# An allocation order that moves a decode kernel's large buffer by 128 bytes

## The chip, the cores and the metric

The kernel runs on one core of one Trainium2 chip. The metric is the device time of one execution in microseconds. SBUF, the core's working memory, has 128 partitions; an address below is a byte offset within each partition, and a tile lies at the same offset in all of its partitions. HBM is the main memory, where inputs and outputs are. Engines: PE multiplies matrices, DVE and ACT do elementwise work, POOL and SP here mainly issue transfers. Transfers are carried by 16 DMA engines, whichever engine issues them.

## The reference

One decode step (one token) of a transformer block, forward and backward, in bfloat16. x and h are vectors of 448 elements.

```
h   = x + A(layernorm(x))          # 16 heads of 256 over 8 K/V heads, window of the last 4096 of 32768 positions, then wo
h2  = h + B(layernorm(h))          # (x @ w_gate) * (x @ w_up) @ w_down, 448 -> 1792 -> 448
outputs: h2, and for grad_out the gradients of x, k_cache, v_cache, wq, wo, w_gate, w_up, w_down
```

The gradients of k_cache and v_cache have the caches' shape, (1, 8, 32768, 256) each, and are zero outside the window of 4096. Writing these zeros is most of what the kernel moves.

## The kernel before

**Memory.** Three pools are opened: `const`, `small` and one in PSUM. Tiles of `const` are laid out one after another in the order in which the code allocates them. The first is `BIG` (L53), 128 x 88,832 bfloat16, 177,664 bytes in each partition, which is 694 x 256. It is cut by hand: ten slots of 16,384 bytes (`SLOT` elements; `slot(k)` and `half(k, h)`, L117 to L121) and a tail of 13,824 bytes. K, V, the weights, the products on their way and the results on their way out all live in BIG at some time. The second is `zeros` (L65), 16,384 bytes in each partition. Then come `Mt` (L110), the identity and mask tiles, the layernorm tiles, `qT`, `pT_all` (L306) and `oT_f` (L307): 32 float32 to a partition, 128 bytes. In the program as built, BIG starts at byte 16,512 of each partition (64.5 x 256), zeros at 194,176 (758.5 x 256), oT_f at 222,432, and the last tile ends 256 bytes below the top of SBUF.

**Transfers.** SP issues the two loads of wq (L64) and then the fills (`fill`, L71): a fill takes 16 of the zero rows, in partitions 32 to 92 by steps of 4, and writes each of them many times over, 16,384 bytes (`ZW` elements) a row, to the region of an output that lies outside the window. There are 15 such fills for whole regions (L76 to L79). The last region is dealt out in pieces (`deal`, `deal_all`, `deal_rest`), the last of them by POOL. All other transfers are issued by POOL (`IO`): loads of K and V rows (16,384 bytes to a partition, or halves of 8,192; `load_window`, L144), of weights (`load_wo`, `load_wd`, L461, L491), and stores of the finished K and V gradients (L730) and weight gradients (`outer`, L618). Fills and POOL's transfers share the 16 DMA engines.

**Work.** For each of the 8 K/V heads g, `moments(g)` (L375) multiplies K rows by the softmax weights and accumulates products with V in PSUM, with the next head's scores between; at its end L410 writes four columns of oT_f. After the loop, L479 reads oT_f (forward output projection), and L582 reads it again in the backward part. The last loop (L702) forms the gradients of K and V head by head, writes them into slots of BIG and stores them. The order of this work is that of the code, with the loads ordered by `io_load` (L137).

Of the kernel before, what the change touches and what calls it, by code (L numbers as in the profile page):

```python
# [8 lines left out]
f32 = mybir.dt.float32  # L9
# [31 lines left out]
def kernel(  # L41
# [7 lines left out]
    const = ctx.enter_context(tc.tile_pool(name="const", bufs=1))  # L49
    small = ctx.enter_context(tc.tile_pool(name="small", bufs=1))  # L50
    ps = ctx.enter_context(tc.tile_pool(name="ps", bufs=1, space=bass.MemoryType.PSUM))

    BIG = const.tile([128, SIZE], bf16)  # L53
    x_bf = BIG[0:1, 6 * SLOT:6 * SLOT + D]
    S_.dma_start(out=x_bf, in_=A_x.rearrange("a b d -> (a b) d"))
    go_bf = BIG[0:1, 6 * SLOT + 512:6 * SLOT + 512 + D]
    S_.dma_start(out=go_bf, in_=grad_out.rearrange("a b d -> (a b) d"))
# [3 lines left out]

    wq_sb = BIG[:, 4 * SLOT:4 * SLOT + NI * HQ]
    for c0, c1 in ((0, 4 * HQ), (4 * HQ, NI * HQ)):
# [53 lines left out]
    def slot(k):  # L117
        return BIG[:, k * SLOT:(k + 1) * SLOT]

    def half(k, h):  # L120
        return BIG[:, (2 * k + h) * SLOT // 2:(2 * k + h + 1) * SLOT // 2]  # L121

# [181 lines left out]
        S_.activation(out=dst, in_=t[:], func=ACT.Copy, scale=scale)  # L304

    pT_all = const.tile([128, G, T, 2], bf16)  # L306
    oT_f = const.tile([128, 32], f32)  # L307
    kbar = const.tile([128, 32], f32)
    dh2_bc = const.tile([128, D], bf16)
    d_hh = const.tile([128, FC], f32)  # L310
# [4 lines left out]
    def ring(k):  # L315
        return BIG[:, SIZE - (k + 1) * 1024:SIZE - k * 1024]

# [448 lines left out]
```

## Time and profile before

| | us |
|---|---|
| median of 3 runs | 788.1 |
| lowest and highest of them | 788.04, 788.3 |
| the profiled execution | 786.81 |
| its span, from first to last instruction | 784.9 |

The profile is of one execution. A line of its third part gives, for each DMA queue, the number of packets, the megabytes, and the time that the packets took as a share of 16 DMA engines over the span. The same lines can be had for any stretch of the span; the share is then of 16 engines over that stretch. Of the queues, q1 is the one that SP feeds, q0 the one that POOL feeds; q8 and q14 fetch instructions. A transfer of one contiguous row is one packet here, but for short rows, of which two can form one. The completion of a transfer is told by packets of 4 bytes. A table of stages gives the busy time of each engine in a stretch, the granted clock of PE as a share of full speed, the busy share of the DMA engines, and GB/s.

### The profile page before, as it was taken

How to read it: one execution, taken by the hardware profiler on the slowest of the kernel's cores; microseconds unless marked ns; L12 is line 12 of the kernel's file. 1: busy time of each engine (PE TensorE's matmuls, PEld its weight loads, DVE VectorE, ACT ScalarE, POOL GpSimd, SP SyncE). 2: the span in 40 equal slices, each digit the busy share in tenths (PEclk: the TensorE clock that was granted, in tenths of full speed). 3: DMA queues.
4: the chain of work that ended last, by engine and by line, in shares of the span. 5: the costliest groups of instructions: out<-in, count | busy, mean ns of one | idle time of the engine just before them, and what ended most of it. 6: DMA issues, size and time to landing. Idle time of an engine off the chain costs nothing.

```text
span 784.9 us, 10845 instructions
## 1 busy us (share of the span) xinstructions
PE 472.8 (60%) x4375; PEld 263.8 (34%) x4420; DVE 401.5 (51%) x1169; ACT 188.5 (24%) x277; POOL 42.3 (5%) x86
## 2 busy tenths in 40 slices
PE   4798898899998631313258897639392889700000
PEld 4654564565554320203134343314141334100000
DVE  5477677677767212295724556436856655600000
ACT  0322322321220000126024453315140444400000
POOL 3000000000000000100000001000100000000000
PEclk9998998999999755555555555555555555555555
DMA  9999999999999999999999999999999999999997
GB/s 355 425 427 430 427 425 430 427 425 430 423 430 429 429 430 432 428 428 432 426 431 426 427 426 422 423 411 427 429 413 429 427 423 423 427 421 427 426 426 297
DMA packets 25106, 330.67 MB, mean 421 GB/s; under 512 B 2669, under 2 KB 2671, under 8 KB 4468
## 3 DMA queue, kind: packets, MB, share of 16 engines
q1 hardware_dynamic: 14557, 231.15, 69.4%
q0 software_dynamic: 10496, 98.83, 30.0%
q8 instruction: 34, 0.56, 0.3%
q14 instruction: 15, 0.12, 0.0%
q10 hardware_dynamic: 4, 0.00, 0.0%
HBM read 49.38 MB, written 280.59 MB: 420 GB/s over the span
## 4 chain that ended last, share of the span: by engine, by line
PE 46%; DMA 17%; DVE 15%; issue 7%; ACT 2%; POOL 1%; POOLq 0%; DVEq 0%; ACTq 0%
PE MT L389 14%; PE d_ps L723 10%; PE tr L332 9%; DMA BIG<-in_B_w_down_dram 7%; DMA out_dram<-BIG 6%; DMA BIG<-in_A_wq_dram 3%; DVE BIG L575 2%; PE sT L337 2%; DMA BIG<-in_A_k_cache_dram 2%; DVE BIG L558 1%; PE acc L392 1%; PE acc L395 1%; DVE zeros L406 1%; PE dp L337 1%; DVE BIG L282 1%
## 5 line engine op out<-in xcount | busy, mean ns | idle before, releaser
L389 PE MATMUL MT<-BIG 128*128 128x512 bf16 x467 | 141.7, 412 | 2.0 <-DVE BIG L385 0.2
L385 DVE TENSOR_SCALAR BIG<-BIG,pf 128x256 bf16<-128x256 bf16 x512 | 114.9, 282 | 27.9 <-PE MT L389 24.8
L723 PE MATMUL d_ps<-BIG 32*128 32x512 bf16 x256 | 118.9, 620 | 9.8 <-ACT BIG L718 5.4
L332 PE MATMUL tr<-ident_bf,BIG 128*128 128x128 bf16 x1024 | 117.1, 268 | 1.8 <-DVE Mt L282 0.8
L282 DVE CAST BIG<-d_ps 128x512 bf16<-128x512 f32 x128 | 88.2, 691 | 52.5 <-PE d_ps L723 52.0
L280 ACT COPY BIG<-tr 128x1024 bf16<-128x1024 bf16 x64 | 64.8, 1012 | 161.0 <-PE tr L332 161.0
L332 PEld LDWEIGHTS <-BIG 128*128 128x128 bf16 x1024 | 79.1, 118 | 40.7 <-issue 40.1
L280 ACT CAST BIG<-d_ps 128x512 bf16<-128x512 f32 x128 | 74.8, 587 | 52.7 <-PE d_ps L723 52.7
L282 DVE COPY BIG<-tr 128x1024 bf16<-128x1024 bf16 x64 | 44.3, 692 | 50.1 <-PE tr L332 50.1
L392 PEld LDWEIGHTS <-BIG 128*128 128x128 bf16 x512 | 42.3, 99 | 52.9 <-issue 16.9
L392 PE MATMUL acc<-pT_all,BIG 128*128 128x2 bf16 x512 | 45.0, 164 | 16.6 <-DVE kbar L411 15.0
L337 PEld LDWEIGHTS <-BIG 128*128 128x128 bf16 x1024 | 39.7, 104 | 40.5 <-DVE BIG L282 19.8
L389 PEld LDWEIGHTS <-BIG 128*128 128x128 bf16 x512 | 40.8, 103 | 24.6 <-issue 18.6
L723 PEld LDWEIGHTS <-BIG 32*128 32x128 bf16 x256 | 27.5, 124 | 56.8 <-issue 56.7
L395 PE MATMUL acc<-pT_all,BIG 128*128 128x2 bf16 x512 | 44.3, 164 | 0.0
L395 PEld LDWEIGHTS <-BIG 128*128 128x128 bf16 x512 | 30.1, 96 | 0.9
L506 DVE CUSTOM_DVE_ANT_0 dh_bc<-BIG,dh_bc 128x448 bf16<-128x448 bf16 x14 | 8.7, 625 | 39.5 <-DMA BIG<-in_B_w_down_dram 39.3
L337 PE MATMUL dp<-doT,BIG 128*128 128x2 bf16 x512 | 24.6, 169 | 7.0 <-DVE BIG L282 5.5
L530 PE MATMUL y<-BIG,hh_bf 128*1 128x448 bf16 x14 | 5.9, 566 | 31.5 <-DMA BIG<-in_B_w_down_dram 28.1
L718 ACT CAST BIG<-R_ps 128x512 bf16<-128x512 f32 x8 | 4.7, 585 | 82.9 <-PE R_ps L716 82.9
L337 PE MATMUL sT<-qT,BIG 128*128 128x2 bf16 x512 | 22.5, 165 | 0.8 <-DVE BIG L282 0.6
L640 DVE CUSTOM_DVE_ANT_0 BIG<-BIG,Mt 128x2048 bf16<-128x2048 bf16 x7 | 15.7, 2288 | 12.1 <-DMA BIG<-in_A_wq_dram 12.1
(185 smaller groups left out, 373.0 us busy)
## 6 DMA issues: line engine op xcount, KB each, us to landing
out_dram<-zeros SPq DMA_DIRECT2D x15, 14336.0 KB, 151.1
out_dram<-BIG POOLq DMA_DIRECT2D x16, 2048.0 KB, 38.2
BIG<-in_A_v_cache_dram POOLq DMA_DIRECT2D x8, 2048.0 KB, 23.6
BIG<-in_A_k_cache_dram POOLq DMA_DIRECT2D x12, 1024.0 KB, 14.2
out_dram<-zeros SPq DMA_DIRECT2D x1, 6144.0 KB
out_dram<-BIG POOLq DMA_DIRECT2D x6, 896.0 KB, 42.9
BIG<-in_A_k_cache_dram POOLq DMA_DIRECT2D x2, 2048.0 KB, 24.1
out_dram<-BIG POOLq DMA_DIRECT2D x3, 1024.0 KB, 49.6
```

The costliest lines, as they stand in the source:

```text
L280: S_.copy(out=out, in_=in_)
L282: V_.tensor_copy(out=out, in_=in_)
L332: P_.transpose(tr[:, i, dh, :], x_at(g, 4 * q + i)[:, dh * 128:(dh + 1) * 128], ident_bf[:])
L337: P_.matmul(out_ps[:, 4 * q + i, :], lhsT=xt[:, i, dh, :], rhs=vecT[:, 4 * g + dh:4 * g + dh + 3:2], start=(dh == 0), stop=(dh == 1))
L385: V_.tensor_scalar(out=pk[:, i, h, :], in0=K[:, t, :], scalar1=pf[:, t, h:h + 1], scalar2=None, op0=ALU.mult)
L389: P_.matmul(MT[hf][:], lhsT=v_at(g, t)[:, hf * 128:(hf + 1) * 128], rhs=pk[:, i, :, :].rearrange("p h d -> p (h d)"), start=(t == 0), stop ...
L392: P_.matmul(acc[:, 2 * hf:2 * hf + 2], lhsT=v_at(g, t)[:, hf * 128:(hf + 1) * 128], rhs=pT_all[:, g, t, :], start=(t == 0 and hf == 0), st ...
L395: mm = P_.matmul(acc[:, 4 + dk:7 + dk:2], lhsT=K[:, t, dk * 128:(dk + 1) * 128], rhs=pT_all[:, g, t, :], start=False, stop=(t == T - 1), s ...
L506: V_.tensor_tensor_reduce(out=dh_bc[:], in0=wd_sb[:, m - m0, :], in1=dh2_bc[:], scale=1.0, scalar=0.0, op0=ALU.mult, op1=ALU.add, accum_ou ...
L575: V_.tensor_tensor_reduce(out=wg_sb[:, 0:D], in0=parked.get(b, wo_b(b)), in1=dh_bc[:], scale=1.0, scalar=0.0, op0=ALU.mult, op1=ALU.add, a ...
L640: V_.tensor_tensor_reduce(out=wq2[i], in0=wq2[i], in1=dq_bc[:, i % 2, :], scale=1.0, scalar=0.0, op0=ALU.mult, op1=ALU.add, accum_out=Pq[: ...
L723: mm = P_.matmul(d_ps[:].rearrange("p w d -> p (w d)"), lhsT=rows[32 * k:32 * k + 32, a, :], rhs=R[32 * k:32 * k + 32, :], start=True, sto ...
```

## The change

The tile oT_f is allocated ahead of BIG and no longer behind pT_all. Nothing else in the code differs, and no instruction uses it earlier or later than before. Its 128 bytes now come first in the pool, so BIG, zeros and the tiles from Mt to pT_all begin 128 bytes further on: BIG at 16,640 (65 x 256) and zeros at 194,304 (759 x 256). Tiles from kbar on, and the pools behind, stay where they are.

```diff
     ps = ctx.enter_context(tc.tile_pool(name="ps", bufs=1, space=bass.MemoryType.PSUM))
 
+    oT_f = const.tile([128, 32], f32)
     BIG = const.tile([128, SIZE], bf16)
     x_bf = BIG[0:1, 6 * SLOT:6 * SLOT + D]
...
     pT_all = const.tile([128, G, T, 2], bf16)
-    oT_f = const.tile([128, 32], f32)
     kbar = const.tile([128, 32], f32)
```

## The prediction

> **What bounds the kernel now.** I read the page's first three parts, then the table of stages, then the transfers of single stretches, because a change of addresses alone can only act through whatever sets the end.
>
> ```profile
> span 784.9 us, 10845 instructions
> PE 472.8 (60%) x4375; PEld 263.8 (34%) x4420; DVE 401.5 (51%) x1169; ACT 188.5 (24%) x277; POOL 42.3 (5%) x86
> DMA  9999999999999999999999999999999999999997
> DMA packets 25106, 330.67 MB, mean 421 GB/s; under 512 B 2669, under 2 KB 2671, under 8 KB 4468
> q1 hardware_dynamic: 14557, 231.15, 69.4%
> q0 software_dynamic: 10496, 98.83, 30.0%
> q8 instruction: 34, 0.56, 0.3%
> q14 instruction: 15, 0.12, 0.0%
> HBM read 49.38 MB, written 280.59 MB: 420 GB/s over the span
> ```
>
> No engine is busy for more than 60% of the span, while the 16 DMA engines are at 9 tenths or more in every slice but the last. Queue 1 holds the zero fills that SP issues and the first weight loads, queue 0 everything that POOL issues. The stages say the same with the engines beside it (columns: stretch, length, busy time of PE, PEld, DVE, ACT and POOL with their instructions, granted clock, DMA share, GB/s):
>
> ```profile
> 0.00:20.00 20.00, 8.58 (x43) 8.36 (x44) 11.61 (x29) 1.59 (x3) 6.02 (x20) 1.00 0.92 356
> 20.00:640.00 620.00, 425.69 (x4139) 240.09 (x4181) 362.96 (x1100) 163.65 (x237) 32.26 (x59) 0.68 1.01 427
> 640.00:690.00 50.00, 38.57 (x196) 15.38 (x196) 26.94 (x41) 23.26 (x38) 3.38 (x6) 0.50 1.01 423
> 690.00:770.00 80.00, 0.00 (x0) 0.00 (x0) 0.00 (x0) 0.00 (x0) 0.63 (x1) 0.50 1.01 427
> 770.00:784.90 14.90, 0.00 (x0) 0.00 (x0) 0.00 (x0) 0.00 (x0) 0.00 (x0) 0.50 0.60 252
> ```
>
> From 20 to 770 us the DMA engines are full (share 1.01; a little over 1 because one packet's record overlaps the next). The compute engines do nothing after 690 us; what remains is transfers. So about 95 us separate the last arithmetic from the end, and the end comes when the bytes are out. Time is the number of rows times the time per row, over 16 engines.
>
> **The change part by part.** No instruction, transfer, wait or loop is added, removed or reordered: the same tile is allocated earlier. Two things follow, addresses on the DMA side and addresses on the engine side.
>
> *Engine side.* BIG, zeros and the tiles after them up to pT_all lie 128 bytes further on, with unchanged shapes and distances within each tile. I cost this at nothing. What hides it is the transfers that run on after 690 us: an engine's work would have to grow by tens of microseconds to reach the end. Without that cover, each 1% on DVE's 401.5 us would be 4 us.
>
> *DMA side.* Practically every row of data that this kernel moves has one end in BIG or in zeros, at 128 bytes past a multiple of 256 (BIG starts at byte 16,512 of each partition, and all the large offsets into it are multiples of 256). Afterwards these ends lie on multiples of 256. The question is whether a row pays for its misplaced start. The trace has no row of this size that is known to be placed otherwise, so I bound the cost from both sides by what a row costs beyond its bytes. Four stretches, each with one size alone on queue 0: 16,384-byte loads of K and V (40 to 43 us), 12,544-byte weight loads (252 to 262), 5,376-byte stores (399 to 403), and the 4-byte completion marks (769 to 779).
>
> ```profile
> q0 software_dynamic: 40, 0.66, 50.9%
> q1 hardware_dynamic: 39, 0.64, 49.7%
> ```
> ```profile
> q0 software_dynamic: 114, 1.43, 33.4%
> ```
> ```profile
> q0 software_dynamic: 80, 0.43, 25.8%
> ```
> ```profile
> q0 software_dynamic: 46, 0.00, 0.3%
> ```
>
> The last column is the share of 16 engines over the stretch, so a row takes share x 16 x length / count:
> - 16,384 B: 0.509 x 48 us / 40 = 610.8 ns for loads; 0.497 x 48 / 39 = 611.7 ns for the fills on queue 1 beside them.
> - 12,544 B: 0.334 x 160 us / 114 = 468.8 ns.
> - 5,376 B: 0.258 x 64 us / 80 = 206.4 ns.
> - 4 B: 0.003 x 160 us / 46 = 10.4 ns, and with the rounding of the share 8.7 to 12.2 ns.
>
> The second and third give a slope of (468.8 - 206.4) / 7,168 = 0.0366 ns a byte and a fixed part of 206.4 - 5,376 x 0.0366 = 9.6 ns a row. Put into the same line, 16,384 bytes come to 609 ns, as seen. Hence the bounds:
> - Upper: a row that starts in the middle of a 256-byte block touches 65 blocks where 64 would do, and carries half a block, 128 bytes, for nothing: 128 x 0.0366 = 4.7 ns. The fixed 9.6 ns has room for that.
> - Lower: nothing. The fixed part belongs to a packet of any kind. The 4-byte marks, which can't carry 128 wasted bytes in this sense, also take about 10 ns.
>
> The number of rows is 25,106 - 2,669 under 512 bytes - 34 - 15 of instruction fetch = 22,388. The upper price gives 22,388 x 4.7 / 16 = 6.6 us. If only rows read from SBUF pay (written to HBM: 280.59 of 329.97 MB, 85%), it is 5.6 us. Below nothing is not excluded by the rows either: the row's mean in a stretch of fills alone is a little above the 611 ns of the clean stretch, and that part could grow. In 412 to 444 us
>
> ```profile
> DMA packets 847, 13.66 MB, mean 427 GB/s; under 512 B 13, under 2 KB 13, under 8 KB 13
> q1 hardware_dynamic: 845, 13.63, 100.1%
> q8 instruction: 2, 0.03, 0.4%
> ```
>
> there are 832 fill rows at 1.001 x 512 us / 832 = 616 ns, 4.3 ns more than 611.7. So the ends are -6.6 us (all rows pay now and stop paying) and +6.0 us (that excess doubles: 4.3 x 22,388 / 16).
>
> I take -6.0 us, between the two ways of counting who pays. I choose the price over nothing since the 9.6 ns is on every row in proportion to rows and not bytes, which is where such a cost would sit, and since with DMA full for 750 us whatever a row saves arrives at the end undiminished. I do not think the trace settles it: loads, whose SBUF end is the destination, and fills, whose SBUF end is the source, cost the same, so either both ends pay alike or neither does.
>
> [...]
>
> **The sum.** The profiled execution took 786.81 us, 1.9 us more than its span of 784.9; the median of the runs is 788.1, 1.3 us above it. 786.81 - 6.0 = 780.8, and 1.3 more gives 782.1 us for the median. Nothing takes the place of the saved time: the next bound is the arithmetic at 690 us.
>
> **The rivals.**
>
> *The start costs nothing.* The 9.6 ns is the price of any packet. For it: the 4-byte marks, and loads and fills alike. Against it: only that no aligned row of this size is there to compare. The time stays at 788.1, with less than 0.2% (1.6 us, about what a measurement of this kernel can tell from no change, 786.5 to 789.7) either way. A layout that is not as the change says would come to the same.
>
> *The rows collide.* Now a row's SBUF end and its HBM end are half a block out of step. Once both are in step, the 16 engines open their blocks together, and the excess over the clean row grows. The place is the stretches where fills and stores run side by side; there the excess exists already, as in 669 to 674 us:
>
> ```profile
> q0 software_dynamic: 65, 1.06, 49.9%
> q1 hardware_dynamic: 65, 1.06, 49.9%
> ```
>
> 0.499 x 80 us / 65 = 614.2 ns for stores and fills alike. It decides from 1.2 ns on the mean row (1.2 x 22,388 / 16 = 1.7 us); with the excess doubled it costs 6.0 us and gives 794.1. For it: the excess is real and varies by stretch. Against it: no row ties it to the place of a start, and the cleanest stretch has loads and fills mixed.
>
> *More than the half block.* If the excess of 4.3 ns itself comes of the misplaced start and goes too, another 6 us fall away: 776 us. For it: the excess is on fills alone too. Against it: the stretch of 40 to 43 us has hardly any, with the same starts.
>
> **How the numbers follow.** The forecast, 781 to 783.5 us: 0.50. Nothing: 0.32. Collision: 0.14. More than the half block: 0.04. Faster by over 0.2% is the first and the last together, 0.54; within 0.2% is 0.32; slower 0.14. The range leaves out the last two cases, whose chances add up to 0.18: it goes from 779.5, a little beyond the upper price, to 789.5, the upper edge of no change. The likeliest case's own range is 781 to 783.5.
>
> **What would show it.** With the forecast, the 40 loads and 39 fills of a clean stretch take about 606 ns a row instead of 611, the 5,376-byte stores 202 instead of 206, the share of queue 1 falls by some 0.7% of itself for the same 231.15 MB, and the GB/s of 20 to 640 us rise from 427 to about 430. If only rows read from SBUF pay, fills fall and loads stay. With the rival of no cost, every one of these rows keeps its duration. With the collision, the clean rows keep 611 and the means of the stretches rise above 616. The prediction is wrong if the fixed part of a row stays at 9 to 10 ns; the 4-byte marks should not move in any case.

## The result, and the profile after

The changed kernel takes 779.34 us (median of 4 runs, 779.24 to 779.54) beside 788.2 for the kernel before in its 4 runs (788.04 to 789.26): ratio 0.9885 with a 95% interval of 0.9868 to 0.9902. It is faster by 8.9 us. The forecast was 6.0, and 779.34 lies 0.16 us below the range. The direction was right and the size too small. The mechanism, as it turns out, is another one than the forecast's: the boundary of 256 bytes matters (779.2 to 779.3 us with both tiles on it, 788.2 to 789.1 with both off it, by the two kernels and three of the experiments), but not by a cost that each row carries (a clean row of 16,384 bytes takes 611 ns before and after), so that the number came out near the range is luck.

The changed kernel's page, the lines that answer to those shown of before:

```profile
span 777.7 us, 10890 instructions
DMA  9999999999999999999999999999999999999998
DMA packets 25106, 330.67 MB, mean 425 GB/s; under 512 B 2669, under 2 KB 2671, under 8 KB 4468
q1 hardware_dynamic: 14557, 231.15, 69.6%
q0 software_dynamic: 10496, 98.83, 30.2%
q8 instruction: 34, 0.56, 0.3%
```

The packets and bytes are the same to the last one. Each share is of a shorter span: queue 1's packets took 0.694 x 784.9 = 544.7 us per engine before and 0.696 x 777.7 = 541.3 now, queue 0's 235.5 and 234.9. So the rows themselves took 4.0 us less, of which 3.4 on queue 1 (a share has one decimal, so each of the four products is good to 0.4 us). The records of the single packets, added up, give 4.7 us less, of which 3.6 on queue 1. The stages (columns as in the prediction):

```profile
20.00:640.00 620.00, 431.73 (x4206) 241.84 (x4204) 365.08 (x1105) 167.28 (x243) 32.25 (x59) 0.68 1.01 429
640.00:690.00 50.00, 33.17 (x177) 13.25 (x174) 23.97 (x36) 19.66 (x33) 4.00 (x7) 0.50 1.01 430
690.00:770.00 80.00, 0.00 (x0) 0.00 (x0) 0.00 (x0) 0.00 (x0) 0.00 (x0) 0.50 1.01 430
```

The DMA engines are as full as before, at 429 to 430 GB/s in place of 427, 423 and 427. Engine work is unchanged; it ends before 690 us as it did.

**A single row costs what it did.** Three stretches of the changed kernel with one size alone on queue 0: 16,384-byte loads (40 to 43 us, with fills beside them), 12,544-byte loads (250 to 260), 5,376-byte stores (396 to 400):

```profile
q1 hardware_dynamic: 38, 0.62, 48.4%
q0 software_dynamic: 38, 0.62, 48.4%
...
q0 software_dynamic: 113, 1.42, 33.1%
...
q0 software_dynamic: 85, 0.46, 27.4%
```

By share x 16 x length / count these are 611.4 ns for loads and fills alike, 468.7 and 206.3. Before they were 611, 468.8 and 206.4. The fixed 9.6 ns of a row did not move by more than the rounding of these shares.

**What moved is the mean of the fill rows late in the run.** For a mixed stretch I take the time of one fill row as share x 16 x length / (bytes / 16,384), good to about 0.5 ns here. Queue 1 of the kernel before in four stretches, 320 to 360, 440 to 500, 520 to 560 and 690 to 750 us:

```profile
q1 hardware_dynamic: 854, 13.73, 80.1%
...
q1 hardware_dynamic: 1041, 16.76, 66.0%
...
q1 hardware_dynamic: 641, 10.24, 59.9%
...
q1 hardware_dynamic: 1018, 16.38, 64.3%
```

and of the changed kernel in 440 to 500 and 690 to 750 us:

```profile
q1 hardware_dynamic: 1028, 16.53, 64.4%
...
q1 hardware_dynamic: 1038, 16.71, 64.9%
```

Before: 611.7, 619.4, 613.4, 617.4 ns. After: 612.8 and 610.9. The excess over the clean 611 comes, goes and comes again in the kernel before, and between 690 and 750 us, where no compute engine works, the change removes all of it.

After 400 us the fill rows are slowest where a load from HBM comes in among the stores. Two loads of wq do so in the second half, issued at 503.5 and 555.0 us; their rows stand below, under the last experiment. Queue 1 in 500 to 520 us, before and after:

```profile
q1 hardware_dynamic: 329, 5.36, 67.6%
```
```profile
q1 hardware_dynamic: 336, 5.49, 64.0%
```

These are 661 and 611 ns a row. By the records of single packets, the excess of queue 1's 16,384-byte rows over 611 ns adds up to 5.7 us per engine before and 2.0 now, and 1.7 of the 3.7 between them falls in the 61.5 us in which these two loads are under way (23.2 and 38.3). In 20 to 400 us, with the loads of K, V and most weights, the two kernels are alike: 613.1 and 613.6 ns.

**The engines also end together.** The last stretches of the kernel before:

```profile
770.00:775.00 5.00, 0.00 (x0) 0.00 (x0) 0.00 (x0) 0.00 (x0) 0.00 (x0) 0.50 0.95 404
775.00:780.00 5.00, 0.00 (x0) 0.00 (x0) 0.00 (x0) 0.00 (x0) 0.00 (x0) 0.50 0.66 281
780.00:784.90 4.90, 0.00 (x0) 0.00 (x0) 0.00 (x0) 0.00 (x0) 0.00 (x0) 0.50 0.17 68
```

and of the changed kernel:

```profile
765.00:770.00 5.00, 0.00 (x0) 0.00 (x0) 0.00 (x0) 0.00 (x0) 0.00 (x0) 0.50 0.98 420
770.00:775.00 5.00, 0.00 (x0) 0.00 (x0) 0.00 (x0) 0.00 (x0) 0.00 (x0) 0.50 0.80 341
775.00:777.70 2.70, 0.00 (x0) 0.00 (x0) 0.00 (x0) 0.00 (x0) 0.00 (x0) 0.50 0.08 31
```

The idle part, (1 - share) x length summed, is 0.25 + 1.7 + 4.1 = 6.0 us of the mean engine before and 0.1 + 1.0 + 2.5 = 3.6 now. That is 2.4 us less of idle engines. I read it so: the excess falls on the 16 engines unequally, and the slowest one sets the end. The trace does not name the engine of a packet, so this is not shown. With the 4.7 us of the rows it makes 7.1 of the span's 7.2. That the medians lie 8.9 apart and the profiled executions 7.3 (786.81 and 779.54) is because the profiled execution of before was 1.4 us under its median.

### The profile page after: what moved, and what is told of

Its sections match the earlier page's. It is cut to its first block, busy times and chain, and to the rows that moved or that the text cites. A ratio compares the mean times of both kernels' runs of the same rounds, so it can differ in the third digit from the quotient of the medians.

```text
span 777.7 us, 10890 instructions
## 1 busy us (share of the span) xinstructions
PE 473.5 (61%) x4420; PEld 263.5 (34%) x4420; DVE 400.7 (52%) x1169; ACT 188.5 (24%) x277; POOL 42.3 (5%) x86
## 4 chain that ended last, share of the span: by engine, by line
PE 47%; DMA 17%; DVE 14%; issue 7%; ACT 2%; POOL 1%; POOLq 0%; DVEq 0%; ACTq 0%
PE MT L389 15%; PE d_ps L723 10%; PE tr L332 9%; DMA BIG<-in_B_w_down_dram 7%; DMA out_dram<-BIG 6%; DMA BIG<-in_A_wq_dram 2%; DVE BIG L575 2%; PE sT L337 2%; DMA BIG<-in_A_k_cache_dram 2%; PE acc L395 1%; DVE BIG L558 1%; DVE zeros L406 1%; PE dp L337 1%; PE acc L392 1%; DVE BIG L283 1%
## 5 line engine op out<-in xcount | busy, mean ns | idle before, releaser
L389 PE MATMUL MT<-BIG 128*128 128x512 bf16 x512 | 148.4, 406 | 0.0
L389 PEld LDWEIGHTS <-BIG 128*128 128x128 bf16 x512 | 40.4, 102 | 23.2 <-issue 16.0
```

Source lines behind the costliest of these rows:

```text
L389: P_.matmul(MT[hf][:], lhsT=v_at(g, t)[:, hf * 128:(hf + 1) * 128], rhs=pk[:, i, :, :].rearrange("p h d -> p (h d)"), start=(t == 0), stop ...
```

## The experiments

All of them are the kernel before or the changed one with one edit; times stand beside runs of the kernel before on the same chip. The row that each is judged by is queue 1 in 690 to 750 us, unless another stretch is named.

**Which tile it is.** One tile of 128 bytes moves between the two large ones (`zeros_only`), or one in front of each, so that BIG alone is on a multiple of 256 (`big_only`).

```diff
# zeros_only, against the kernel before
+    oT_f = const.tile([128, 32], f32)
     zeros = const.tile([128, ZW], bf16)
# big_only, against the changed kernel
+    kbar = const.tile([128, 32], f32)
     zeros = const.tile([128, ZW], bf16)
```

> BIG stays at 128 past a multiple of 256, zeros alone moves onto one (194,304 = 759 x 256). Theory 1 (a row suffers when its SBUF end starts off a 256-byte boundary, by slower rows in the loaded stages after 400 us): the fills on queue 1 lose their excess (their mean from 617.5 to about 613 ns as in the changed kernel, 3.7 us of the 4.7 us summed per engine), rows between BIG and HBM keep theirs; time about 781 to 782 us. Theory 2 (rows hinder each other, so that any misplaced traffic slows all rows beside it): the excess on both queues falls in part wherever stores run; time 782 to 786. Theory 3 (the gain is an accident of how the engines' streams fall against each other, not of a start): no order is expected; time may lie anywhere from 776 to 790.

> BIG on a multiple of 256 (16,640), zeros at 128 past one (194,432). Theory 1: fills keep their excess (mean near 617 ns on queue 1), stores from BIG lose theirs; time 786 to 787.5 us. Theory 2: partial fall on both queues, 782 to 786. Theory 3: anything from 776 to 790. If theory 1 holds, the two gains of this run and of the run with zeros alone add up to about 8.9 us.

Measured: 780.61 us (ratio 0.9905, 0.989 to 0.9919) and 786.47 (0.9975, 0.9966 to 0.9984) beside 788.5. First zeros alone, then BIG alone:

```profile
q1 hardware_dynamic: 1030, 16.58, 64.5%
```
```profile
q1 hardware_dynamic: 1030, 16.58, 64.8%
```

The fill rows take 611.9 and 614.7 ns. zeros alone brings 7.9 us, BIG alone 2.0; together 9.9, near the 8.9 of both. So the gain belongs to the two tiles' places, and most of it to zeros, from which nearly all of queue 1's 231 of 331 MB leave. By these two times alone theory 3 is not out, since its range takes in both; the offsets below speak against it. That the fills lose 2.7 of their 6.4 ns when only BIG, which they do not read, moves speaks for theory 2: misplaced rows slow the rows beside them. The other run says the same. With zeros alone moved, the 16,384-byte rows of queue 0 in this stretch, most of them stores from the BIG that is still misplaced, fall from 615.8 to 611.4 ns by their packets' records. Theory 1 would have kept them slow, and the time at 781 to 782 us.

**Which places are good.** Three other offsets, made by allocating other small tiles first: 192 past a multiple of 256, 32 past one, and on a multiple of 512.

```diff
# off192, against the kernel before; its later allocation goes
+    d_hh = const.tile([128, FC], f32)
     BIG = const.tile([128, SIZE], bf16)
# off32, against the changed kernel; its later allocation goes
+    eps_t = const.tile([128, 1], f32)
     BIG = const.tile([128, SIZE], bf16)
# al512, against the changed kernel; their later allocations go
+    kbar = const.tile([128, 32], f32)
+    oW = const.tile([128, 32], f32)
     BIG = const.tile([128, SIZE], bf16)
```

> Both tiles at 192 past a multiple of 256 (BIG 16,576, zeros 194,240). Theory 1 in the form of wasted bytes (the bytes ahead of the start count, 192 here and 128 before): worse than before, excess of the rows about 1.5 times, time 790 to 793 us. Theory 1 in the form of the extra block (65 blocks for 64, whatever the offset): like before, 787 to 789. A rule of 64 bytes in place of 256 (64 is a multiple of 64): like the changed kernel before it would be if 128 were harmless, so 128 and 192 would be alike and the rule is refuted by the change itself. Theory 3: anything from 776 to 790.

> Both tiles at 32 past a multiple of 256 (BIG 16,672, zeros 194,336). If the bytes ahead of the start count (32 here, 128 before): a quarter of the loss, 781 to 782 us. If only the extra block counts: as before, 788 to 789. If 32 or 64 bytes were the step that counts, 128 would have cost nothing; the change itself refutes that.

> Both tiles on multiples of 512 (BIG 16,896, zeros 194,560), where the changed kernel has them on odd multiples of 256. If 256 is the step that counts: as the changed kernel, 779.3 us within 0.5. If 512 counts too: faster still, by up to the excess left on queue 1 (613.3 against 611 ns, 2 us): 777 to 778. Theory 3: anything from 776 to 790.

Measured: 789.14 us at 192 (ratio 1.0013, 1.0004 to 1.0022), 789.07 at 32 (1.0001, 0.9992 to 1.0011), 779.16 at 512 (0.9887, 0.987 to 0.9903). Their fill rows, in the same order:

```profile
q1 hardware_dynamic: 1014, 16.32, 64.2%
```
```profile
q1 hardware_dynamic: 1013, 16.30, 64.2%
```
```profile
q1 hardware_dynamic: 1033, 16.63, 64.6%
```

These are 618.7, 619.5 and 611.0 ns. Offsets of 32, 128 and 192 cost the same within 0.2%, so the bytes ahead of the start do not count by their number. 512 brings nothing over 256. Where a start lies, and not a chance order of streams, decides: the two places on a boundary are fast, the three off it slow.

**Place or stage.** The fills in reverse order of heads, on the kernel before.

```diff
-    for g in range(G):
+    for g in reversed(range(G)):
         for o in (out_2, out_3):
```

> The kernel before with the 15 whole-region fills in the reverse order of heads, both tiles still at 128 past a multiple of 256. In the kernel before, the mean of the fill rows is 611 to 616 ns up to 400 us and lies above 615 in most of the stretches after it. Theory place (the excess belongs to the HBM region that the rows go to): the slow rows move to the first 400 us and the late stretches are near 612. Theory stage (it belongs to what runs beside: the loads of the first half spare the rows, the stores of the second half do not): the rows after 400 us stay above 615, those before stay near 613. Time within 1 us of 788 in both.

Measured: 788.83 us (1.0004, 0.9995 to 1.0014). Queue 1 in 100 to 200 us and in 440 to 500:

```profile
q1 hardware_dynamic: 1725, 27.74, 65.1%
...
q1 hardware_dynamic: 1044, 16.83, 66.4%
```

615.2 and 620.5 ns, where the kernel before has 613.3 and 619.4; in 690 to 750 us it is 618.4. In the first of these stretches the runs differ without the change too (the changed kernel has 615.0 there). The slow rows stay where they were in time, so the HBM region is not what makes them slow.

**One end or the difference of both.** The whole-region fills, shifted by 128 bytes in HBM, on both kernels, and a reference without a shift on the kernel before. All three leave out one row in 56 of these fills, so parts of the outputs stay unwritten.

```diff
# hbm_shift_b and hbm_shift_a; hbm_ctl_b has 0 in place of 64
-                fill(FILL, region(o, g), ALL, 8 * NZ, ZW)
+                r = region(o, g).rearrange("(p x) -> p x", p=16)[:, 64:64 + 55 * ZW]
+                FILL.dma_start(out=r.rearrange("p (n f) -> p n f", f=ZW), in_=zeros[ALL, :].unsqueeze(1).to_broadcast([16, 55, ZW]))
```

> The kernel before (SBUF ends at 128 past a multiple of 256), its 15 whole-region fills shifted by 128 bytes in HBM, so that both ends of a fill row lie at 128 past; each of the 16 parts writes 55 rows where it wrote 56, and 128 bytes ahead of them are left out too, so some 9 us less of rows are moved. Theory SBUF start: the excess stays, the mean of the fill rows on queue 1 between 400 and 780 us as in the kernel before, 616 to 620. Theory step (only the difference between the two ends counts): the excess is gone, mean about 612 in these stretches.

> The changed kernel (SBUF ends on multiples of 256) with the same shift of its fills by 128 bytes in HBM and the same rows left out. Theory SBUF start: no excess, fill rows at 611 to 613 ns between 400 and 780 us. Theory step: the excess is there, 616 to 620. If HBM has a start of its own that counts: the excess is there in this run and in the other one.

> The kernel before with the last of 56 rows of each part of the whole-region fills left out, without a shift in HBM: the reference for the two runs with a shift. 240 rows fewer are 240 x 611 / 16 = 9.2 us: time 778 to 780 us, and the mean of the fill rows on queue 1 as in the kernel before, 617.5 ns within 1.

Measured, one time each: 780.37 us (both ends off), 774.71 (HBM end off), 779.41 (SBUF end off, the reference). Queue 1 in 412 to 444 us, a stretch of fills alone, in this order, and then of the changed kernel:

```profile
q1 hardware_dynamic: 842, 13.53, 100.0%
```
```profile
q1 hardware_dynamic: 844, 13.57, 100.3%
```
```profile
q1 hardware_dynamic: 851, 13.68, 100.5%
```
```profile
q1 hardware_dynamic: 850, 13.71, 100.3%
```

These are 620.0, 620.0, 616.3 and 613.7 ns. Moving both ends alike does not help, so the difference between the ends is not what counts. Against my expectation for the SBUF start alone, an HBM end off the boundary makes an excess of its own, a smaller one in 690 to 750 us: there the three runs have 618.6, 613.7 and 617.6 ns, and the changed kernel 610.9. Its price in time is 774.71 against 779.34 - 9.2 for the rows left out, 4.6 us. Where the SBUF end is off already, 780.37 against 779.41 tells nothing: single runs of the kernel before lie between 787.41 and 789.73.

**The extra block or the start.** Rows cut by 128 bytes, so that a misplaced row too touches 64 blocks of 256 bytes in SBUF. The last 128 bytes of each row's place in HBM stay unwritten.

```diff
# short_b on the kernel before, short_a on the changed one
-                fill(FILL, region(o, g), ALL, 8 * NZ, ZW)
+                r = region(o, g).rearrange("(p n f) -> p n f", p=16, f=ZW)[:, :, 0:ZW - 64]
+                FILL.dma_start(out=r, in_=zeros[ALL, 0:ZW - 64].unsqueeze(1).to_broadcast([16, 56, ZW - 64]))
```

> The kernel before (SBUF ends at 128 past a multiple of 256); each row of its 15 whole-region fills is cut to 16,256 bytes, and the last 128 bytes of each 16,384 in HBM are left out. A row still starts in the middle of a block, but ends on a boundary and touches 64 blocks. Theory extra block (the 65th block makes the excess): most fill rows at their clean time of about 606 ns in all stretches after 400 us, mean within 2 ns of it as in the changed kernel. Theory start (a start off the boundary makes it, whatever the end): the mean stays 4 to 8 ns above the clean time in these stretches. Rows are 0.8% shorter, so the time falls by some 4 us in either case and says little alone.

> The changed kernel with the same shorter rows: start on a boundary, end 128 bytes before one, 64 blocks. Theories extra block and start: no excess, mean within 2 ns of the clean 606 ns after 400 us. If the rows of HBM with their gaps make an excess of their own, it shows here and is to be taken off the other run.

Measured, one time each: 783.46 and 779.79 us, beside 788.72 for the kernel before. Rows of 16,256 bytes, short_b first:

```profile
q1 hardware_dynamic: 1033, 16.44, 64.2%
```
```profile
q1 hardware_dynamic: 1032, 16.45, 63.9%
```

609.4 and 606.2 ns. An excess of 3 ns stays with 64 blocks, against 6 in the kernel before, and 3.7 us between the two times, against 8.9. Neither theory is met whole: the start alone costs, in this stretch at about half the price. BIG is misplaced in short_b too, so part of the 3 ns may come from the rows beside. Nor is the pair clean. In 412 to 444 us the two runs are alike, at 610.2 and 610.4 ns, both above the clean 606, and short_a is no faster than the changed kernel, though its shorter rows should have spared some 4 us. So these rows, or the gaps that they leave in HBM, have a price of their own, and what the extra block costs stays open.

**What sets the stage.** One more load late in the kernel before.

```diff
         for job in side[s]:
             job()
+        if s == 6:
+            IO.dma_start(out=slot_kv(2), in_=A_k_cache[0, 0, Sk - W:, :].rearrange("(p t) d -> p t d", t=T))
```

> The kernel before with one more load, 2 MB of K into a slot that is free by then, issued after the seventh head's stores; what it loads is not used. Theory drift (misplaced rows fall into each other's way bit by bit while only writes to HBM run, and reads from HBM part them again, as the clean stretch right after the wq loads near 520 us suggests): the share of fill rows at the clean 611 ns, about 0.3 in 680 to 780 us of the kernel before, rises to 0.9 while the load runs and for some 30 us after it. Theory stage (it depends on what is stored or on the time alone): the share stays at 0.2 to 0.4. The load's own 128 rows cost 4.9 us; time 791 to 793.

Measured: 796.47 us, one time, beside 788.72. The trace has the load's issue at 647.5 us and its landing 38.0 us later:

```profile
L734 POOL DMA_DIRECT2D BIG<-in_A_k_cache_dram x1: 535/535/535, 647.5 to 647.5; - x1
DMA to landing us min/median/max: 38.0/38.0/38.0
```

Queue 1 in 640 to 670 us, 690 to 730 and 750 to 780:

```profile
q1 hardware_dynamic: 532, 8.49, 69.7%
...
q1 hardware_dynamic: 613, 9.83, 57.3%
...
q1 hardware_dynamic: 634, 9.69, 75.9%
```

646 ns while the load is under way, 611.2 for 40 us after it has landed, and 616.0 again later. The kernel before has 620.0, 617.1 and 616.9 in these stretches. In 690 to 730 us all 600 fill rows of queue 1 took 611 ns by their records (a share of 0.9 was expected), beside 31% of the rows in the kernel before. The tiles lie as badly as before, and yet the rows are clean for a while. My reading is that a read from HBM parts what has run together, after which it runs together anew. One run does not show that it is the read: POOL issued the load ahead of the sixth head's stores and not behind the seventh's, and while it waited for the slot these stores were held up too, from 635.7 us in the kernel before to 648.0. Much the same is to be seen without an edit in the kernel before, at 613.4 ns in 520 to 560 us, behind the first part of wq, which this fence of its trace shows issued at 503.5 us and landed after 23.2 (the second at 555.0, after 38.3):

```profile
L636 POOL DMA_DIRECT2D BIG<-in_A_wq_dram x2: 532/532/532, 503.5 to 555.0; - x2
...
DMA to landing us min/median/max: 23.2/30.8/38.3
```

The load costs more than it spares: 7.8 us, of which its 128 rows explain 4.9. The time of 791 to 793 that I expected had no room for the slow rows while it runs.

## Why the prediction was wrong

- *What bounds the kernel:* right. The end is set by rows, and neither the engine side nor a new wait took anything of the gain (in the changed kernel no compute engine works after 690 us, and the DMA share is 1.01 from 20 to 770 us).
- *The price of a row:* this step failed. I took 4.7 ns for half a block of 256 bytes that each row carries, an estimate of mine from the slope of 0.0366 ns a byte, and found room for it in the fixed 9.6 ns. No run shows a row that carries such bytes, nor that rows are moved in blocks. The fixed part is the same in aligned rows (611, 468.7 and 206.3 ns against 611, 468.8 and 206.4). The 4.7 ns would have shown in these clean rows, and a price by the bytes ahead of the start as a loss that grows with the offset; neither is there. What the runs showed in its place is that the three offsets cost alike (789.07, 788.2 and 789.14 us at 32, 128 and 192 past a multiple of 256, 779.34 and 779.16 on one), and that the price stands in the means of the later stretches (617.4 ns against 610.9 in 690 to 750 us). The rival "the start costs nothing" had this half right: the fixed part is about what the 4-byte marks take (9.6 ns beside 10.4 in the kernel before, by a share that is good to 1.7).
- *The excess over the clean row:* this step failed too. I left it in place, as a thing of its own, and gave 0.04 to a case in which it goes. It is what went: 6 ns a row between 690 and 750 us, 50 ns a row in 500 to 520 us. My argument against was that the clean stretch at 40 us has the same starts. That holds for a cost that belongs to a row, not for one that arises among rows: the fills' excess shrinks when only BIG moves (617.4 to 614.7 ns). Why the first 400 us are spared is not shown. That it builds up while little is read from HBM is a reading that the run with the late load agrees with (611.2 ns for 40 us behind it) and does not show.
- *The rival of collisions* had a collision in it, with the wrong sign: the rows hinder each other when they start off the boundary (with zeros alone moved, queue 0's rows fell from 615.8 to 611.4 ns), and the mean in 412 to 444 us fell from 616 to 613.7 ns where this rival had it rise.
- *Time as rows divided by 16:* the sum took the engines as equal. The last transfers ran out with 2.4 us less of idle engines, which the sum did not have.
- *What would show it:* the GB/s of 20 to 640 us rose to 429, near the 430 that I named, by another route. The clean rows, which I named as the test, spoke against me.

What stays open is where the rows meet (HBM, the way to it, or SBUF's side), since an end off the boundary on either side makes an excess (in 690 to 750 us 617.4 ns with the SBUF end off, 613.7 with the HBM end off, 610.9 with neither); why rows with 64 blocks keep half of it (3 ns against 6); and why misplaced rows are so slow while a load runs among stores (661 and 646 ns) and clean behind it (613.4 and 611.2).

## What to carry to other kernels

Where transfers set the end, place both ends of long rows on multiples of 256 bytes; here a tile of 128 bytes moved in the pool was worth 1.1% (788.2 to 779.34 us), 32 bytes off cost as much as 128 (789.07 beside 788.64), and the HBM ends of the fills 128 bytes off some 4.6 us in a single run. A mean row time that differs between stretches, beside a clean one that doesn't, can be a cost among rows, which a clean stretch can't rule out. Here it stood late, in stretches of stores (617.4 and 619.4 ns against 611), and most of all where a load came in among them (661). Look at the drain as well: its idle engines added 2.4 us to the 4.7 of the rows.

## What the runs showed of the hardware that was not expected

- Misplaced fill rows cost nothing that shows in the first 400 us, with the loads of K and V (613.1 ns in 20 to 400 us, 613.6 when placed well), 6 to 8 ns where stores run for long (619.4 in 440 to 500 us, 617.4 in 690 to 750), and 50 ns where a load of wq comes in among the stores (661 against 611 in 500 to 520 us).
- One 2 MB load among stores was followed by some 40 us without an excess (617.1 to 611.2 ns), after 646 ns while it was under way.
- With both tiles on multiples of 256 or 512 the times scatter less: 779.24 to 779.54 and 779.12 to 779.20 us in 4 runs each, against 788.04 to 789.26 for the kernel before in its 4 runs and 787.07 to 789.47 in the 19 beside the first experiments.
